# A fused attention and MLP kernel: weight splits tied to the MLP's steps, value halves at later steps

## The chip, the cores and the metric

One core of one Trainium2 chip runs the whole program. The metric is the device time of one launch in microseconds (us), and lower is better. The engines are named as in the profile: PE (TensorE matmuls), DVE (VectorE), ACT (ScalarE), POOL (GpSimd) and SP, which issues the transfers. Each engine works through its own instructions in the order in which they stand, so one that waits holds up all that stand behind it.

## What is computed

Attention within clusters: a query sees only those keys that the same centroid wins. Its result goes through a two-layer MLP with a squared ReLU.

```python
# q, k, v: (4, 8, 768, 64); centroids: (8, 16, 64); x: 3072 tokens of 512
q_n, k_n, c_n = (t / (norm(t) + 1e-6) for t in (q, k, centroids))
q_assign = argmax(einsum('bhsd,hcd->bhsc', q_n, c_n), -1)      # k_assign likewise
mask = q_assign[:, :, :, None] == k_assign[:, :, None, :]
attn = softmax(where(mask, q @ k.T / sqrt(64), -1e9))
x = (attn @ v) laid out as (3072, 512)
h = x @ w_in                                # w_in: 512 x 2048
out = (s * relu(h) ** 2 + b) @ w_out        # w_out: 2048 x 512
```

## The kernel before

To keep float32 accuracy on float16 matmuls, a tensor is split into a high half (the value rounded to float16) and a low half (what rounding left), and the products of the halves are added up in PSUM.

**The loop.** The main loop counts steps `i`. Attention has 192 units; a unit is one batch, one head and 128 queries against 768 keys. Step `i` makes the scores of unit `i` on PE (L516), their maximum on DVE (L526) and their exponentials on ACT (L536). Units 0 to 15 (`RAW`) are multiplied with unsplit values: PE transposes their exponentials (L560), and ACT and DVE copy the result out of PSUM (L140, L142). From unit 16 on `high` and `low` split the exponentials, the low half on POOL (L568), a transposing DMA turns them (L570), and `value` multiplies them with the value halves four steps later (L617 to L619). After 16 units a chunk of 256 tokens is complete (`finish_x`), and the MLP works on it 21 steps (`LAG`) behind: step `i` runs MLP step m = i - 21, that is pair `ft` = m mod 16 of chunk m div 16. `mlp_in` (L676) multiplies with the first layer's weights of that pair, `mlp_relu` takes the sum out of PSUM with ACT (L683, L685, L686), `mlp_gl` makes a low half on POOL (L691), and three steps on `mlp_out` (L703) multiplies with the second layer's weights.

**The weights.** 32 pieces of 512 KB (16 of each layer) are loaded in the first steps by `weights`: the load (SP, into three buffers called `stage` and a fourth place called `gs`), `rebase` (ACT, L244), `narrow` (DVE, L248 and L249), and `bound` (ACT, L256 and L258, and PE, L261), which gathers norms. When all 32 are through, `finish_w_in` and `finish_w_out` make the scales in `glob`, and only then `wsplit(ft)` can split pair `ft`: for each of its two tiles (`wis`, `wos`) ACT writes the high half (L307) and DVE the low half (L310). A split writes into one of 33 buffers, of which five are free at first, so the later splits wait for the low half of an earlier one, with which a raw weight's buffer comes free. `wsplit(ft)` is started in step 17 + ft.

**The value halves.** `prep_v(0)` splits the first batch's values, a pair of heads at a time (`halves`): ACT the high half (L223), DVE the low half (L225). The pair `hp` is let in from step 14 + 2 hp (`RAW - 2 + 2 * hp`), and first read at step 20 + 4 hp. The unsplit values stay in their buffers (`kv`, five in all) until then.

**What sets the order.** The functions only record instructions. A list scheduler with a timeline of its own puts them in order, engine by engine: what was recorded earlier goes first unless it isn't ready in that timeline, then something later fills in. `behind(x)` puts what is recorded under it behind `x` on the engine of `x`; it sets order and adds no wait for the end of `x`. `first_of_all` lifts the units 0 to 19 above the rest. In `wsplit` the pairs from `ft` = 4 on stand behind `first_x`, the last instructions of `finish_x` for the fourth group of units; the first four stand behind nothing.

## Time and profile before

| | us |
|---|---|
| median of 3 runs | 911.07 (909.8 to 915.86) |
| the profiled execution, its own time | 912.4 |
| its span, first to last instruction | 910.7 |
| PE busy | 830.3 (91%) |
| ACT busy | 712.7 (78%) |
| DVE busy | 631.2 (69%) |
| POOL busy | 544.0 (60%) |

The shares are averages over a start (some 220 us, in which the weights come in and the engines other than PE are full) and a long rest in which PE is nearly always busy. The page also shows that TensorE's clock was granted in full from 157.8 us on and was at times at half before. A time is read as microseconds from the span's start. "Busy" is the union of an engine's instruction times in a stretch; the idle time in brackets behind a row is that of its engine just before it, with what ended it.

### The profile page before, as it was taken

What the parts mean: (1) busy time and instruction counts of PE and PEld (TensorE: products, weight loads), DVE (VectorE), ACT (ScalarE), POOL (GpSimd) and SP (SyncE); (2) the same over time, 40 slices, a digit from 0 to 9 for tenths busy, and PEclk for the clock granted to TensorE, in tenths of its full rate; (3) what the DMA queues carried; (4) which work ended last, traced back from release to release, by engine and by line L of the source; (5) the groups of instructions that cost most, each with busy time, mean ns of one, the idle gap of its engine ahead of it and who ended that gap; (6) DMA issues with size and microseconds to landing.
All of it is one profiled execution on the core that took longest, in us unless ns stands there. A gap on an engine that the chain in (4) does not pass through costs nothing.

```text
span 910.7 us, 22840 instructions
## 1 busy us (share of the span) xinstructions
PE 830.3 (91%) x8625; PEld 591.9 (65%) x8625; DVE 631.2 (69%) x1673; ACT 712.7 (78%) x1406; POOL 544.0 (60%) x580
## 2 busy tenths in 40 slices
PE   1675786899999899999999999999999999999997
PEld 0564664566677667777667767677677777777764
DVE  8789789979778758766877667669777557564200
ACT  4579786867798779889888788988988788788553
POOL 3111024587687668768778667777876667676422
PEclk9977576999999999999999999999999999999999
DMA  5997624697998897989899989689988767676200
GB/s 151 245 287 239 205 49 91 163 178 163 182 181 140 182 209 139 175 158 180 175 180 190 181 152 185 154 150 207 177 156 171 140 124 173 117 149 132 59 24 23
DMA packets 437758, 144.23 MB, mean 158 GB/s; under 512 B 405392, under 2 KB 434064, under 8 KB 437648
## 3 DMA queue, kind: packets, MB, share of 16 engines
q1 hardware_dynamic: 437648, 142.78, 76.1%
q8 instruction: 67, 1.10, 0.5%
q14 instruction: 43, 0.35, 0.1%
HBM read 35.69 MB, written 6.29 MB: 46 GB/s over the span
## 4 chain that ended last, share of the span: by engine, by line
PE 44%; DVE 21%; DMA 14%; ACT 9%; issue 6%; POOL 3%; SPq 2%; DVEq 0%; ACTq 0%; POOLq 0%
PE h L676 15%; PE acc L703 14%; PE sc L516 7%; DMA kn<-in_k_dram 4%; DVE ssm L526 4%; DMA qn<-in_q_dram 4%; ACT p L536 2%; PE sc L617 2%; PE sc L619 2%; ACT ssm L533 2%; PE sc L618 2%; DMA vn<-in_v_dram 2%; DVE ka L225 2%; SPq L570 1%; POOL ph L568 1%
## 5 line engine op out<-in xcount | busy, mean ns | idle before, releaser
L568 POOL TENSOR_TENSOR ph<-p,ph 128x768 f16<-128x768 f32 x176 | 296.3, 1683 | 154.0 <-ACT ph L140 63.9
L676 PE MATMUL h<-xk,wis 128*128 128x256 f16 x2304 | 288.3, 274 | 5.1 <-DMA xk<-xn 2.3
L703 PE MATMUL acc<-wos,gs 128*128 128x512 f16 x1152 | 280.6, 379 | 2.0 <-DVE o L711 0.8
L676 PEld LDWEIGHTS <-wis 128*128 128x128 f16 x2304 | 222.9, 98 | 63.6 <-issue 6.3
L536 ACT ACTIVATE p<-sc,ssm,qsm 128x768 f32<-128x768 f32 x192 | 189.3, 986 | 4.3
L526 DVE TENSOR_REDUCE ssm<-sc 128x1 f32<-128x768 f32 x192 | 181.9, 947 | 6.3 <-PE sc L516 6.2
L691 POOL TENSOR_TENSOR gs<-r,gs 128x256 f16<-128x256 f32 x192 | 136.1, 710 | 64.3 <-ACT r L686 55.3
L703 PEld LDWEIGHTS <-gs 128*128 128x128 f16 x1152 | 104.4, 98 | 94.8 <-issue 1.1
L533 ACT ACTIVATE ssm<-ssm,lift,qsm 128x1 f32<-128x1 f32 x192 | 73.0, 381 | 83.2 <-DVE ssm L526 82.5
L140 ACT ACTIVATE ph<-p 128x768 f16<-128x768 f32 x164 | 137.2, 836 | 0.6
L683 ACT ACTIVATE r<-h,cf 128x256 f32<-128x256 f32 x192 | 89.1, 465 | 39.8 <-PE h L676 34.0
L617 PE MATMUL sc<-halves,PT 128*128 128x65 f16 x1032 | 113.0, 195 | 0.1
L618 PE MATMUL sc<-halves,PT 128*128 128x64 f16 x1032 | 112.9, 192 | 0.0
L619 PE MATMUL sc<-halves,PT 128*128 128x65 f16 x1032 | 112.6, 193 | 0.0
L516 PE MATMUL sc<-keys,QA 128*128 128x384 f16 x384 | 99.8, 341 | 12.8 <-ACT p L536 10.9
L516 PE MATMUL sc<-keys,QB 128*128 128x384 f16 x384 | 99.7, 341 | 8.3 <-DMA QB<-qb 8.3
L617 PEld LDWEIGHTS <-PT 128*128 128x128 f16 x1056 | 99.0, 97 | 11.9 <-DMA PT<-ph 0.8
L618 PEld LDWEIGHTS <-PT 128*128 128x128 f16 x1056 | 98.1, 99 | 11.6 <-issue 0.7
L619 PEld LDWEIGHTS <-PT 128*128 128x128 f16 x1056 | 98.3, 97 | 0.0
L686 ACT ACTIVATE r<-r 128x256 f32<-128x256 f32 x192 | 79.2, 413 | 4.0
L623 DVE TENSOR_SCALAR ssm<-sc 128x1 f32<-128x1 f32 x172 | 26.3, 153 | 80.5 <-PE sc L619 79.0
L685 ACT ACTIVATE gs<-r 128x256 f16<-128x256 f32 x192 | 78.6, 411 | 1.6
(191 smaller groups left out, 1104.7 us busy)
## 6 DMA issues: line engine op xcount, KB each, us to landing
wst<-in_moe_w_in_dram SPq DMA_DIRECT2D x16, 512.0 KB, 4.7
kn<-in_k_dram SPq DMA_DIRECT2D x16, 384.0 KB, 4.2
qn<-in_q_dram SPq DMA_DIRECT2D x24, 256.0 KB, 3.6
vn<-in_v_dram SPq DMA_DIRECT2D x16, 384.0 KB, 3.9
out_dram<-o SPq DMA_DIRECT2D x12, 512.0 KB, 3.3
wst<-in_moe_w_out_dram SPq DMA_DIRECT2D x8, 512.0 KB, 5.0
gs<-in_moe_w_out_dram SPq DMA_DIRECT2D x8, 512.0 KB, 5.8
PT<-ph SPq DMA_TRANSPOSE x176, 3.5
```

Source lines behind the costliest of these rows:

```text
L140: A.activation(dst, src, AF.Copy)
L516: last_score[0] = nc.tensor.matmul(sc[:, e, :HALF], X[:, col, :], y[:, h * S + e * HALF : h * S + (e + 1) * HALF], start=st, stop=not st)
L526: last_max[0] = V.tensor_reduce(SM[i // 4][:, 0, j : j + 1], U[i]["sc"], axis=AX.XY, op=ALU.max, negate=True)
L533: A.activation(bi, sm[:, 0, j : j + 1], AF.Identity, scale=u["scale"], bias=lift)
L536: last_exp[0] = A.activation(p.rearrange("p (a b) -> p a b", a=2), u["sc"], AF.Exp, bias=bi, scale=u["scale"], **total)
L568: G.tensor_tensor(u["ph"][:, 1, :], u["p"], u["ph"][:, 0, :], op=ALU.subtract)
L617: nc.tensor.matmul(o1, PT[:, kt, :], vh[:, h, kt, : D + 1], start=(kt == 0), stop=False)
L618: nc.tensor.matmul(o, PT[:, kt, :], vl[:, h, kt, :], start=False, stop=False)
L619: nc.tensor.matmul(o1, PT[:, T + kt, :], vh[:, h, kt, : D + 1], start=False, stop=(kt == T - 1))
L676: nc.tensor.matmul(ph[:, :CW], WSP[ft][0][:, wl, kt, :], XS[(b, c, kt)][:, :, xl, :], start=(i == 0), stop=(i == len(terms) - 1))
L691: G.tensor_tensor(g[:, 1, :], r, g[:, 0, :], op=ALU.subtract)
L703: nc.tensor.matmul(acc[:, t, :], g[:, gl, rows], WSP[ft][1][:, wl, :], start=(ft == 0 and gl + wl == 0), stop=(ft == NF - 1 and gl == 1))
```

## The change

Four things change.

1. The pairs from `ft` = 4 on: the high halves (ACT) stand behind the latest `mlp_relu` recorded (`last_relu`), the low halves (DVE) behind the latest maximum (`last_max`). Since `wsplit(ft)` starts in step 17 + ft and goes on in the next two, `wis` stands behind the relu of pair ft - 4 of the first chunk (ACT) and the maximum of unit 18 + ft (DVE), and `wos` one step behind it.
2. The pairs 1 to 3 stand behind the two copies that take the last unsplit unit's transposes out of PSUM (`last_copy`).
3. The value halves of the first batch are let in at the steps 16, 19, 22 and 25, behind the latest exponentials and the latest maximum.
4. The queries of the second half of the heads of chunk 1 are loaded into a `stage` buffer, no longer into one of the eleven `big` ones.

```diff
--- before.py
+++ after.py
@@ -73,7 +73,8 @@
 
 
     last_transpose = [None]
-    first_x = [None, None]
+    last_relu = [None]
+    last_copy = [None, None]
     last_turn = [None]
     last_qa = [None]
     last_qb = [None]
@@ -137,9 +138,8 @@
 
     def copy(eng, dst, src):
         if eng is A:
-            A.activation(dst, src, AF.Copy)
-        else:
-            eng.tensor_copy(dst, src)
+            return A.activation(dst, src, AF.Copy)
+        return eng.tensor_copy(dst, src)
 
     def scalar_in(src, name):
         every = const([P, 1], F32, name)
@@ -303,10 +303,10 @@
         made = []
         for w, f in ((wi[ft], glob[:, 2:3]), (wo[ft], glob[:, 5:6])):
             e = parts(weight_tile(f"w{'io'[len(made)]}s{ft}"))
-            with behind(*first_x[: 2 * (ft >= 4)]):
+            with behind(*([last_relu[0]] if ft >= 4 else last_copy if ft else ())):
                 A.activation(e[:, 0], w, AF.Copy, scale=f)
             yield
-            with behind(*first_x[: 2 * (ft >= 4)]):
+            with behind(*([last_max[0]] if ft >= 4 else last_copy if ft else ())):
                 V.scalar_tensor_tensor(e[:, 1], w, f, e[:, 0], op0=ALU.mult, op1=ALU.subtract)
             made.append(e)
         WSP[ft] = (made[0], made[1].rearrange("p e a f -> p e (a f)"))
@@ -392,7 +392,7 @@
     def prep_q(b, c, hq):
         n = f"{b}_{c}_{hq}"
         nh = 4
-        if b or c > 1:
+        if b or c > 1 or c + hq > 1:
             qn = sb.tile([P, CT * DM], F32, tag="stage", name=f"qn_{n}", bufs=3)
         else:
             qn = sb.tile([P, T * P], F32, tag="big", name=f"qn_{n}", bufs=BIGN)
@@ -479,7 +479,7 @@
         V.tensor_scalar(vm[:, 6:7], vm[:, 6:7], 2.0 ** -19, None, op0=ALU.mult)
         for hp in range(NP):
             if b == 0:
-                yield from until(RAW - 2 + 2 * hp)
+                yield from until(RAW + 3 * hp)
             if b == 1 and hp == 0:
                 yield from until(LAG + NF - 1)
             both = halves[:, (b * NP + hp) % 5]
@@ -487,7 +487,12 @@
             vl = both[:, VHW:].rearrange("p (h t d) -> p h t d", h=2, t=T)
             VS[(b, hp)] = (vh, vl)
             G.memset(vh[:, :, :, D:], 1.0)
-            yield from split(vh[:, :, :, :D], vl, vns[hp], vm[:, 7:8], False)
+            parted = split(vh[:, :, :, :D], vl, vns[hp], vm[:, 7:8], False)
+            with behind(*((last_exp[0], last_max[0]) if b == 0 else ())):
+                next(parted)
+            yield
+            with behind(*((last_exp[0], last_max[0]) if b == 0 else ())):
+                next(parted, None)
             if hp < NP - 1:
                 yield
                 if b > 0:
@@ -560,7 +565,9 @@
                     nc.tensor.transpose(turned[:, e, kt * P : (kt + 1) * P], u["p"][:, (e * n + kt) * P : (e * n + kt + 1) * P], ident)
                 cols = slice(e * n * P, (e + 1) * n * P)
                 if i < RAW:
-                    copy((V, A)[e], flat[:, cols], turned[:, e, : n * P])
+                    done = copy((V, A)[e], flat[:, cols], turned[:, e, : n * P])
+                    if i == RAW - 1:
+                        last_copy[e] = done
                 else:
                     A.activation(two[:, 0, cols], turned[:, e, : n * P], AF.Copy)
                     V.tensor_tensor(two[:, 1, cols], turned[:, e, : n * P], two[:, 0, cols], op=ALU.subtract)
@@ -636,9 +643,8 @@
         if hp == 0:
             XM[(b, c)] = sb.tile([P, 8], F32, tag="xm", name=f"xm_{g}", bufs=4)
         xn = sb.tile([P, CT, 2, 2, D], F16, tag="xn", name=f"xn_{g}", bufs=1)
-        made = [A.activation(xn[:, :, 0], xs, AF.Copy), absmax(XM[(b, c)][:, hp : hp + 1], xs.rearrange("p t h d -> p (t h d)"))]
-        if g == NP - 1:
-            first_x[:] = made
+        A.activation(xn[:, :, 0], xs, AF.Copy)
+        absmax(XM[(b, c)][:, hp : hp + 1], xs.rearrange("p t h d -> p (t h d)"))
         yield
         G.tensor_tensor(xn[:, :, 1], xs, xn[:, :, 0], op=ALU.subtract)
         x = xs_kept[:, g % 9]
@@ -680,7 +686,7 @@
         n = f"{b}_{c}_{ft}"
         ph = GS[(b, c, ft)]
         r = sb.tile([P, CW], F32, tag="r", name=f"r_{n}", bufs=2)
-        A.activation(r, ph[:, :CW], AF.Relu, scale=MS[(b, c)][0])
+        last_relu[0] = A.activation(r, ph[:, :CW], AF.Relu, scale=MS[(b, c)][0])
         g = gs[:, ft % 4]
         A.activation(g[:, 0, :], r, AF.Square)
         A.activation(r, r, AF.Square)
```

Nothing is computed otherwise than before. Where the instructions stand now, at three places:

ACT in the middle of the weights' preparation, before. `xs_0` and `xs_1` are results of the first units, `wo9`, `wi8` and so on are weight pieces, `wab` the work of `bound`, `PT_8` a copy of transposed exponentials:

```order
L635 ACTIVATE xs_0_663<-xs_0_663,vm_0_318 128x256
L223 ACTIVATE halves_131<-vn_0_0_319,vm_0_318 128x12x64
L223 ACTIVATE halves_131<-vn_0_1_443,vm_0_318 128x12x64
L223 ACTIVATE halves_131<-vn_0_2_511,vm_0_318 128x12x64
L223 ACTIVATE halves_131<-vn_0_3_588,vm_0_318 128x12x64
L244 ACTIVATE wo9_843<-gs_128 128x512
L140 ACTIVATE PT_8_916<-turned_138 128x384
```

and with the change:

```order
L642 ACTIVATE xs_0_663<-xs_0_663,vm_0_318 128x256
L244 ACTIVATE wo9_843<-gs_128 128x512
L141 ACTIVATE PT_8_916<-turned_138 128x384
L258 ACTIVATE wab_16_885<-wi8_790 128x512
L642 ACTIVATE xs_1_879<-xs_1_879,vm_0_318 128x256
L646 ACTIVATE xn_0_776<-xs_0_663 128x2x128
L256 ACTIVATE wab_17_899,l1_133<-wo8_798 128x512
```

The four high halves of the values are gone from here, and `wo9` with all behind it moves up by four instructions; on DVE the four low halves leave the same place.

ACT behind the exponentials of unit 18, before (`p_18`: exponentials, `wis4`, `wos4`: high halves of weights, `qb_0_1_1`: queries, `ssm`: bias of a maximum):

```order
L536 ACTIVATE p_18_1376<-sc_18_1367,ssm_16_1303,qsm_0_1_0_819 128x768
L533 ACTIVATE ssm_16_1303<-ssm_16_1303,lift_136,qsm_0_1_0_819 128x1
L223 ACTIVATE qb_0_1_1_1362<-qn_0_1_1_1222,qsm_0_1_1_1262 128x4x64
L639 ACTIVATE xn_3_1397<-xs_3_1332 128x2x128
L307 ACTIVATE wis4_1577<-wi4_542,glob_134 128x512
L307 ACTIVATE wos4_1634<-wo4_550,glob_134 128x512
L307 ACTIVATE wis5_1640<-keys_130,glob_134 128x512
L307 ACTIVATE wos5_1700<-keys_130,glob_134 128x512
L307 ACTIVATE wis6_1705<-keys_130,glob_134 128x512
L307 ACTIVATE wos6_1781<-wo6_684,glob_134 128x512
L307 ACTIVATE wis7_1785<-wi7_722,glob_134 128x512
L536 ACTIVATE p_19_1428<-sc_19_1419,ssm_16_1303,qsm_0_1_0_819 128x768
```

and with the change:

```order
L541 ACTIVATE p_18_1373<-sc_18_1364,ssm_16_1300,qsm_0_1_0_819 128x768
L646 ACTIVATE xn_3_1394<-xs_3_1329 128x2x128
L223 ACTIVATE qb_0_1_1_1359<-qn_0_1_1_1220,qsm_0_1_1_1259 128x4x64
L541 ACTIVATE p_19_1423<-sc_19_1414,ssm_16_1300,qsm_0_1_0_819 128x768
L223 ACTIVATE halves_131<-vn_0_1_443,vm_0_318 128x12x64
L538 ACTIVATE ssm_20_1465<-ssm_20_1465,lift_136,qsm_0_1_0_819 128x1 x2
L541 ACTIVATE p_20_1468<-sc_20_1436,ssm_20_1465,qsm_0_1_0_819 128x768
L689 ACTIVATE r_0_0_0_1555<-h_0_0_0_1542,cf_0_0_1538 128x256
L141 ACTIVATE ph_20_1528<-p_20_1468 128x768
L541 ACTIVATE p_21_1532<-sc_21_1502,ssm_20_1465,qsm_0_1_0_819 128x768
L307 ACTIVATE wis4_1571<-wi4_542,glob_134 128x512
L689 ACTIVATE r_0_0_1_1618<-h_0_0_1_1605,cf_0_0_1538 128x256
```

Seven weight splits stood between `p_18` and `p_19`. Now `p_19`, `p_20`, the first relu (`r_0_0_0`) and `p_21` come ahead of the first of them, and one pair stands there in each step.

DVE from the maximum of unit 27 to that of unit 28, before (all weights are split by then; `xs_6` is a unit's result, `vm_1` and `ka_1_0` are work on the next batch's values and keys):

```order
L526 TENSOR_REDUCE ssm_24_1747<-sc_27_1943 128x1
L119 TENSOR_REDUCE vm_1_1702<-vn_1_2_1859 128x1
L119 TENSOR_REDUCE xm_4_1707<-xs_5_1736 128x1
L225 SCALAR_TENSOR_TENSOR qa_0_2_0_1852<-qn_0_2_0_1636,qsm_0_2_0_1696,qb_0_2_0_1853 128x4x64 x2
L623 TENSOR_SCALAR ssm_24_1747<-sc_28_2017 128x1
L624 RECIPROCAL ssm_24_1747<-ssm_24_1747 128x1
L627 TENSOR_SCALAR xs_6_2042<-sc_28_2017,ssm_24_1747 128x64
L526 TENSOR_REDUCE ssm_28_2052<-sc_28_2017 128x1
```

and with the change:

```order
L531 TENSOR_REDUCE ssm_24_1744<-sc_27_1943 128x1
L310 SCALAR_TENSOR_TENSOR wos8_1939<-wo8_798,glob_134,wos8_1939 128x512
L310 SCALAR_TENSOR_TENSOR wis9_1941<-wi9_835,glob_134,wis9_1941 128x512
L120 TENSOR_REDUCE xm_4_1704<-xs_5_1733 128x1
L630 TENSOR_SCALAR ssm_24_1744<-sc_28_2017 128x1
L120 TENSOR_REDUCE vm_1_1699<-vn_1_3_1935 128x1
L142 CAST ph_27_2050<-p_27_1979 128x768
L631 RECIPROCAL ssm_24_1744<-ssm_24_1744 128x1
L329 TENSOR_REDUCE om_q0_2_0_2095<-pq_0_2_0_2078 128x8
L225 SCALAR_TENSOR_TENSOR ka_1_0_2006<-kn_1_0_1634,ksm_1_0_1855,ka_1_0_2006 128x12x64
L469 TENSOR_REDUCE amb_v1_2348<-vm_1_1699 128x1
L634 TENSOR_SCALAR xs_6_2042<-sc_28_2017,ssm_24_1744 128x64
```

Two weight splits (`wos8`, `wis9`) now stand behind this maximum, and two behind each of the next ones, up to `wos15` behind that of unit 34. Between the maxima of the units 20 and 24 three splits are left on DVE where fifteen stood before.

## Rows read from the trace of the kernel before

**Rows 1.** Windows: busy us (instructions) of PE, PEld, DVE, ACT, POOL; granted clock, DMA.
```profile
72.20:118.40 46.20, 32.23 (x189) 24.66 (x190) 38.74 (x97) 38.83 (x85) 5.43 (x6) 0.63 0.67 205
118.40:142.60 24.20, 16.84 (x111) 13.42 (x111) 21.09 (x60) 16.94 (x31) 9.10 (x8) 0.75 0.20 44
142.60:166.30 23.70, 18.89 (x164) 12.64 (x163) 23.57 (x42) 17.69 (x32) 11.06 (x9) 0.68 0.63 124
166.30:181.90 15.60, 12.55 (x125) 8.42 (x126) 15.60 (x38) 12.63 (x28) 7.71 (x8) 1.00 0.62 151
181.90:199.00 17.10, 15.65 (x190) 10.31 (x189) 14.27 (x32) 11.24 (x23) 13.50 (x14) 1.00 0.89 169
199.00:220.50 21.50, 19.96 (x207) 13.60 (x204) 16.59 (x53) 16.55 (x35) 14.98 (x15) 1.00 0.82 166
220.50:279.00 58.50, 57.85 (x633) 40.13 (x634) 42.39 (x113) 45.38 (x86) 43.69 (x45) 1.00 0.91 174
```

**Rows 2.** Windows of line L310 alone: DVE busy us (instructions), clock, DMA.
```profile
118.40:142.60 24.20, 8.75 (x12) 0.75 0.20 44
142.60:166.30 23.70, 15.14 (x15) 0.68 0.63 124
166.30:181.90 15.60, 5.64 (x6) 1.00 0.62 151
```

**Rows 3.** Timeline, ACT and PE, behind unit 18: start us, us, engine, line, names.
```profile
130.66 0.98 ACT L536 ACTIVATE p<-sc,ssm,qsm 128x768 f32<-128x768 f32 x1
134.32 0.71 ACT L307 ACTIVATE wis<-wi,glob 128x512 f16<-128x512 f32 x1
140.90 0.72 ACT L307 ACTIVATE wis<-wi,glob 128x512 f16<-128x512 f32 x1 [1.52 <-DVE wos L310]
141.53 0.97 ACT L536 ACTIVATE p<-sc,ssm,qsm 128x768 f32<-128x768 f32 x1
142.55 0.80 PE L516 MATMUL sc<-keys,QA 128*128 128x384 f16 x2 [4.28 <-ACT p L536]
```

**Rows 4.** Timeline, value halves on ACT and DVE, then SP's next load.
```profile
79.97 3.40 ACT L223 ACTIVATE halves<-vn,vm 128x768 f16<-128x768 f32 x4
81.97 1.95 DVE L225 SCALAR_TENSOR_TENSOR halves<-vn,vm,halves 128x768 f16<-128x768 f32 x2
88.17 0.52 SPq L91 DMA_DIRECT2D gs<-in_moe_w_out_dram  x1
```

**Rows 5.** Timeline, SP, DVE and ACT around the queries' transpose.
```profile
99.45 1.23 SPq L431 DMA_TRANSPOSE QA<-qa  x1
105.17 0.29 DVE L329 TENSOR_REDUCE om_q<-pq 128x8 f32<-128x128 f32 x1 [1.45 <-PE pq L441]
111.16 0.63 ACT L256 ACTIVATE wab<-wo 128x512 bf16<-128x512 f32 x1 [3.31 <-PE pw L261]
118.37 0.16 DVE L292 TENSOR_REDUCE amb_w<-l 128x1 bf16<-128x16 f32 x1
```

**Rows 6.** Timeline, two splits on DVE and a low half on POOL.
```profile
149.33 0.75 DVE L310 SCALAR_TENSOR_TENSOR wos<-wo,glob,wos 128x512 f16<-128x512 f32 x1
149.65 1.93 POOL L568 TENSOR_TENSOR ph<-p,ph 128x768 f16<-128x768 f32 x1 [9.53 <-ACT ssm L533]
150.19 1.93 DVE L310 SCALAR_TENSOR_TENSOR wis<-wi,glob,wis 128x512 f16<-128x512 f32 x1
```

**Rows 7.** Timeline, PE: one pair's mlp_in at half and at full clock.
```profile
150.88 2.75 PE L676 MATMUL h<-xk,wis 128*128 128x256 f16 x12
164.53 1.47 PE L676 MATMUL h<-xk,wis 128*128 128x256 f16 x12
```

**Rows 8.** Timeline, DVE: queries' low halves, a values' maximum, the maximum of unit 36.
```profile
143.22 0.87 DVE L225 SCALAR_TENSOR_TENSOR qa<-qn,qsm,qb 128x256 f16<-128x256 f32 x2
181.82 0.94 DVE L119 TENSOR_REDUCE vm<-vn 128x1 f32<-128x768 f32 x1
220.51 0.95 DVE L526 TENSOR_REDUCE ssm<-sc 128x1 f32<-128x768 f32 x1
```

## Prediction

> **What bounds the kernel now.** I read the windows first, with bounds at a few DVE instructions [rows 1]: the first is where the weights' scales begin (the maximum over their norms, at 118.37 [rows 5]), the others are the ends of the maxima of the units 20, 24, 27, 31 and 36. The reader should look for the engine that is full. Before 118.4 DVE and ACT are busy 38.7 and 38.8 of 46.2 us. From 118.4 to 181.9 DVE is busy 60.3 of 63.5 us, without a gap in its last 39 us, while PE is busy 48.3 and runs at half clock for much of it. From 181.9 on DVE has slack (30.9 of 38.6), PE is over 90% busy, and from 220.5 to 279.0 PE is busy 57.9 of 58.5. So there are three stages: the weights' preparation, which ACT, DVE and the loads share; a stage that DVE bounds, up to unit 27; and PE's stage, which is the rest of the program. From unit 27 to 36 a step takes (17.1 + 21.5) / 9 = 4.3 us.
>
> What fills DVE is the weight split: of its 60.3 us, 29.5 are L310 (33 entries, one counted twice at an edge, so 0.90 each) [rows 2]. ACT shows the other side of it: between the exponentials of the units 18 (130.66) and 19 (141.53) stand seven high halves, the last of which waits 1.52 us for DVE to free a buffer, and PE waits 4.28 us for unit 19's exponentials [rows 3].
>
> After the maximum of unit 36 both kernels have the same work left, and PE bounds it. I therefore work out when that maximum ends with the change, against 221.46 before (220.51 + 0.95 [rows 8]; the window ends at its start). Every difference there reaches the end in full.
>
> **The weights' preparation.** The change takes four high halves from ACT (3.40 us at 79.97) and four low halves from DVE (two of them 1.95 us at 81.97, so 3.9) [rows 4]. They stood ahead of `wo9`, whose end frees the buffer for the load at 88.17, so that load and the pieces behind it start earlier. Besides, SP issued the queries' transpose QA at 99.45 behind a weight load that waited for DVE; the scores' stage stands still on it, DVE waits 1.45 us for the product made from it at 105.17, and ACT 3.31 us at 111.16 for a norm queued behind it on PE [rows 5]. With the change SP has QA ahead of that load. Lower bound of the gain: 0, if the loads alone set the pace. Upper bound: the 3.9 us of DVE work plus the two waits' larger part, some 6 us. As DVE and ACT are at 84% there, I take nearly the ACT work itself: **3.5 us**, so the scales begin at 114.9. The `stage` buffer for the queries of chunk 1 costs nothing: the weights' last loads are through by then.
>
> **From there to unit 36**, window by window, DVE's work first. A split is 0.73 in the first window (8.75 / 12) and 0.90 later, a value half 0.95 [rows 4], two queries' low halves 0.8 (0.87 with what overlaps the next) and a maximum of the next batch's values 0.9 [rows 8].
> - 118.4 to 142.6, to unit 20: 21.1 busy before. Three splits leave (-2.2), one value half comes (+0.95), two queries' halves come (+0.8), a 0.7 us maximum has moved ahead: 19.9. The splits of pair 3 now stand in the wait for the first chunk's maximum, so 3.1 us of idle time shrink to 1.7: 21.6 us, before 24.2.
> - To unit 24: 23.6 busy before. Twelve of fifteen splits leave (-15.1 + 2.7), two value halves come (+1.9), the queries' go (-0.8): 12.2. DVE is no longer the bound. The four steps are bounded below by PE's pace, 4 x 4.3 = 17.2. From above they are bounded by PE at half clock, at which one `mlp_in` takes 2.75 us against 1.47 [rows 7]: four of them add 5.1, and scores and second layer not more than that again on the four steps that are mixed here: some 23.5. Clock is at half in much of this window before, and PE will be denser: I take 19.0, before 23.7.
> - To unit 27: 15.6 before; as many splits (6); a value half, a values' maximum and two queries' low halves come in (0.95 + 0.9 + 0.8): 18.2. DVE is full again: 18.6 us, before 15.6.
> - To unit 31: 14.3 before; eight splits come (+7.2); the maximum and the queries' halves go (-1.7), small work on keys and values comes from the next window (+1.2): 21.0 in all, with 1.1 idle 22.1 us, before 17.1.
> - To unit 36: 16.6 before; seven splits come (+6.3), that small work and a chunk's first numbers go (-1.6): 21.3, with 1.2 idle 22.5 us, before 21.5.
>
> The sum is 103.8 us against 102.1: 1.7 lost. The reason is plain: DVE's work up to unit 36 is 92.6 us against 91.1 (the splits only move, and the value halves are added), and now it has idle time early, in steps 20 to 24, which the pacing keeps it from filling, while the late steps, which DVE had slack in, become DVE's: 5.0 us a step against PE's 4.3. ACT's part of the splits (0.71 each [rows 3]) fits: 11.2 of 17.1 and 16.6 of 21.5 us were busy there. The splits' lateness costs PE nothing by itself: `wis10`, for one, stands behind the maximum of unit 28, and its first product stands behind the scores of unit 30.
>
> With the 3.5 us gained before, the end moves by **-1.8 us**. Against the profiled execution's own 912.4 us that is 910.6; that execution is 1.3 us above the median, and from the median it is 911.07 - 1.8 = **909.3 us**.
>
> **Price of a split beside POOL.** At 149.33 a low half takes 0.75 us; at 150.19, begun under a POOL low half of 1.93 us, the same takes 1.93 [rows 6]. POOL is busy 47% and 49% of the windows in which most splits stand now, and 79% and 70% of the two in which fifteen of them will stand [rows 1]. The 0.90 that I use holds some such meetings already; the bounds for the fifteen are 0.66 (start to start of splits that meet nothing: -3.6 us in all) and 1.93 (+15.5 us). I stay at 0.90, since a split behind an even unit's maximum comes before POOL's next low half is ready. The Trainium skill ("SBUF — State Buffer", section "Who interferes with whom") has a rule for it that speaks against the change: a DVE instruction with two inputs in SBUF and a GpSimd instruction that reads SBUF share a port, and whichever starts first holds it to its end. The pair of rows agrees with it, and by the rule alone the fifteen late splits would meet POOL more often than the others do, which is the third rival below.
>
> **The rivals.**
> 1. *The slack is used, faster.* Meetings stay rare (-0.24 x 15 = -3.6), steps 20 to 24 run at PE's pace (-1.8), the preparation gains 6 (-2.5), two thirds of the idle time in the last two windows go (-1.5): -9.4 from the forecast, **899.9**. For it: DVE idles 0.1 us in 39 when it is the bound. Against it: each piece must come out at its favourable end.
> 2. *PE's clock holds the early steps.* With the clock at half through steps 20 to 24 the 19.0 become 23.5: **913.8**. For it: clock 0.75 and 0.68 in these windows before. Against it: PE has more to do in a row than before.
> 3. *POOL meets the late splits, slower.* Half of the fifteen wait as at 150.19: 7.5 x 1.03 = +7.7, **917.0**; all of them, 924.8. It decides from about two in three on, where the time passes 1% above now. For it: POOL's 79% and 70%. Against it: at 47 to 49% the price was only some 0.2 per split above the clean one.
> 4. *The preparation isn't shorter*, since loads set it: +3.5, **912.8**, the change then doing in its first part nothing that counts.
>
> **How the numbers follow.** Forecast 0.45 (905 to 913), rival 1 0.23, rival 2 0.10, rival 3 0.12, rival 4 0.10. The range takes in the rivals up to the middle of 1 and of 3: 900 to 917.5. About 1%, 9.1 us, is what a measurement of this kernel can tell from no change: below 902.0 is most of rival 1 (0.18 with a little of the forecast), above 920.2 the far part of rival 3 and mixtures of 2 and 3 (0.08).
>
> **What would show it.** In the changed kernel's profile: the scales begin near 115 (118.4 now); the exponentials of unit 19 follow those of unit 18 within 4 us instead of 10.9; DVE has gaps between the maxima of the units 20 and 24 and almost none from 24 to 36, where a step takes some 5 us; the maximum of unit 36 begins near 219; L310's mean stays near 0.95 us. The forecast is wrong if DVE keeps gaps behind unit 27 (something else bounds, or the sum of its work is less than 92 us), if L310's mean passes 1.3, or if the start gains what I say and the steady steps behind unit 48 differ.

## The result, and the profile after

The changed kernel takes 925.64 us (median of 4 runs, 920.88 to 928.0) against 910.6 beside it: a ratio of 1.0143, interval 1.0114 to 1.0171. A second set of its runs gave 1.0122 (1.0082 to 1.0163). It is slower by 1.2 to 1.4%, where 909.3 us, no measurable change, was forecast. The profiled execution took 920.88 us.

The page after, TensorE's busy time and the clock granted to it in 40 slices:

```profile
PE 827.2 (90%) x8625; PEld 589.4 (64%) x8625; DVE 642.9 (70%) x1673; ACT 712.4 (78%) x1406; POOL 548.7 (60%) x580
PEclk9967689998999999999999999999999999999999
```

PE's busy time is 827.2 us, 3.1 less than before, in a span that is 8.5 longer: PE waits.

The windows of the start, with bounds as in [rows 1] (the scales, then the ends of the maxima of the units 20, 24, 27, 31 and 36):

```profile
72.20:112.40 40.20, 29.79 (x189) 22.67 (x188) 35.41 (x92) 35.76 (x83) 5.01 (x6) 0.69 0.81 236
112.40:132.10 19.70, 15.39 (x131) 12.21 (x130) 18.58 (x58) 13.46 (x23) 8.92 (x8) 0.86 0.24 55
132.10:148.50 16.40, 12.63 (x136) 8.65 (x133) 13.94 (x29) 12.03 (x24) 11.05 (x10) 0.90 0.74 138
148.50:169.90 21.40, 17.70 (x176) 11.86 (x175) 21.26 (x41) 17.12 (x36) 12.32 (x11) 1.00 0.71 166
169.90:190.40 20.50, 17.12 (x206) 11.99 (x205) 20.43 (x42) 16.61 (x32) 14.14 (x14) 1.00 0.59 131
190.40:216.10 25.70, 15.61 (x170) 10.12 (x167) 24.80 (x56) 18.79 (x37) 17.32 (x16) 0.95 0.58 136
```

DVE (the third pair) idles 2.5 us between the maxima of the units 20 and 24 and 1.1 us in all from there to unit 36: the picture that was forecast. Four lines of the timeline answer [rows 5], [rows 3] and [rows 8]: the scales, the exponentials of the units 18 and 19, the maximum of unit 36:

```profile
112.40 0.17 DVE L292 TENSOR_REDUCE amb_w<-l 128x1 bf16<-128x16 f32 x1 [0.68 <-ACT wab L256]
127.01 0.98 ACT L541 ACTIVATE p<-sc,ssm,qsm 128x768 f32<-128x768 f32 x1
128.59 0.99 ACT L541 ACTIVATE p<-sc,ssm,qsm 128x768 f32<-128x768 f32 x1
215.14 0.94 DVE L531 TENSOR_REDUCE ssm<-sc 128x1 f32<-128x768 f32 x1
```

So the start is better than forecast: that maximum begins 5.4 us before the one at 220.51 of [rows 8], where 1.8 were said (3.4 in the mean of the eight profiles below that have this start, against the five with the old one). And yet the end is 8.5 us later. To see where they go I compare, unit by unit, the start of PE's first score matmul (L516, with the change L521; four to a unit) in the profiled executions. Us against before, minus is ahead:

| profile | unit 36 | 42 | 48 | 54 | 84 | 121 | 191 |
|---|---|---|---|---|---|---|---|
| changed kernel | -10.0 | -2.9 | -3.1 | -4.2 | +2.8 | +8.3 | +8.5 |

Before, they start at 217.68, 246.11, 269.10, 293.87, 415.33, 565.72 and 840.98. Two things happen: a lead of ten becomes one of three at once, and between the units 54 and 121 some 12.5 us are lost, steadily and for good. From unit 121 on it hardly changes.

Windows of the first loss, from the scores of unit 36 to those of unit 42, before and then with the change; PE is the first pair after the length, the granted clock the third number from the end:

```profile
217.68:246.11 28.43, 27.23 (x286) 17.49 (x284) 20.85 (x58) 20.68 (x39) 20.45 (x21) 1.00 0.93 192
207.71:243.21 35.50, 29.56 (x294) 19.42 (x292) 27.98 (x66) 23.49 (x44) 22.90 (x23) 0.90 0.80 157
```

Of the 7.1 us between them 4.7 are waits of PE, and 2.3 are PE's busy time: its clock, in full there before, was granted at half (1.2 GHz) from 213.6 to 220.4. It fell within two waits of PE, of 1.56 and 2.82 us, with 0.6 us of products between them (their rows stand with the last experiment).

Windows of the second loss, with bounds at the first scores of the units 54, 66, 75, 87, 105 and 121; PE is the first pair after the length. Before:

```profile
293.87:343.85 49.98, 47.02 (x504) 33.00 (x502) 33.17 (x84) 39.60 (x78) 32.27 (x33) 1.00 0.95 188
343.85:380.57 36.72, 36.72 (x416) 26.66 (x416) 29.93 (x89) 32.64 (x65) 27.34 (x26) 1.00 0.93 170
380.57:426.48 45.91, 45.91 (x530) 32.81 (x528) 28.55 (x87) 40.08 (x79) 35.41 (x35) 1.00 0.82 156
426.48:501.10 74.62, 72.44 (x826) 52.06 (x822) 58.45 (x150) 63.93 (x126) 56.77 (x61) 1.00 0.94 184
501.10:565.72 64.62, 63.21 (x705) 44.79 (x702) 43.27 (x121) 52.59 (x104) 45.63 (x46) 1.00 0.89 166
```

With the change:

```profile
289.68:342.92 53.24, 50.88 (x527) 35.54 (x526) 36.94 (x95) 41.10 (x80) 32.80 (x33) 1.00 0.90 182
342.92:380.49 37.57, 33.51 (x393) 24.22 (x392) 27.61 (x79) 30.93 (x63) 26.98 (x27) 1.00 0.82 159
380.49:428.65 48.16, 45.48 (x506) 32.21 (x504) 29.38 (x83) 38.35 (x75) 33.72 (x34) 1.00 0.74 143
428.65:503.17 74.52, 71.90 (x840) 52.13 (x837) 56.13 (x152) 63.37 (x125) 56.01 (x60) 1.00 0.89 177
503.17:573.99 70.82, 65.20 (x711) 45.46 (x709) 49.69 (x125) 54.53 (x108) 47.42 (x47) 1.00 0.80 166
```

The five add up to 271.9 us with PE idle 6.6, and to 284.3 with PE idle 17.3. Of the 12.5 us that are lost 10.8 are waits of PE; its work is the same within 1.7. Up to unit 66 PE idles no more than before; it only does more of its products early, which are missing in the next windows. The added waits lie behind. Of what PE waits for, the view of waits names, before (294 to 564 us; us in total, times, longest):

```profile
PE sc L516 <- DMA QB<-qb: 2.8, 2, 1.8
PE h L676 <- DMA xk<-xn: 2.3, 1, 2.3
```

and after (290 to 571 us):

```profile
PE h L682 <- ACT r L689: 3.3, 2, 2.7
PE sc L521 <- ACT p L541: 2.4, 4, 1.4
PE pk L386 <- DMA keys<-ka: 2.1, 1, 2.1
PE am_q L116 <- DVE ssm L630: 1.6, 2, 1.0
PE h L682 <- DVE oe_k L330: 1.4, 1, 1.4
```

A few waits for transposes have become many for ACT, DVE and the keys. No line of code of that stretch was changed. But the order of its instructions was: of PE's 3613 matmuls from the scores of unit 40 up to those of unit 121, 581 stand behind another unit's scores than before; from there on the order is the same but for one. For example, what stands on PE behind the scores of a unit, in counts of matmuls (`h`: first layer, `acc`: second, `pq`: queries, `am`: small maxima; the 18 value products left out):

```
unit   before                              changed
61     6 acc, 12 h                         16 pq, 12 h
62     6 acc, 12 h                         10 acc, 21 h
63     6 acc, 12 h                         3 h
64     6 acc, 12 h, 2 am                   2 am, with 14 acc and 12 h between its two halves of scores
71     12 h, 6 acc, 12 h                   1 h, with 11 h ahead of the value products
82     12 h, 8 acc, 2 h, 4 acc             5 acc
```

In the units 61 to 64 an even 18 MLP products each have become bunches and short units. In a short unit PE comes sooner to the next scores or the next `h`, for which ACT must have made room; in these four units that cost a wait of 0.5 us, the longer ones come from unit 69 on.

### The profile page after: what moved, and what is told of

Its sections match the earlier page's. It is cut to its first block, busy times and chain, and to the rows that moved or that the text cites. A ratio compares the mean times of both kernels' runs of the same rounds, so it can differ in the third digit from the quotient of the medians.

```text
span 919.2 us, 22818 instructions
## 1 busy us (share of the span) xinstructions
PE 827.2 (90%) x8625; PEld 589.4 (64%) x8625; DVE 642.9 (70%) x1673; ACT 712.4 (78%) x1406; POOL 548.7 (60%) x580
## 5 line engine op out<-in xcount | busy, mean ns | idle before, releaser
L709 PE MATMUL acc<-wos,gs 128*128 128x512 f16 x1152 | 283.5, 379 | 5.7 <-DVE o L717 2.4
L521 PE MATMUL sc<-keys,QA 128*128 128x384 f16 x384 | 99.3, 339 | 12.3 <-ACT p L541 9.1
L521 PE MATMUL sc<-keys,QB 128*128 128x384 f16 x384 | 99.5, 341 | 7.9 <-DMA QB<-qb 7.9
L625 PEld LDWEIGHTS <-PT 128*128 128x128 f16 x1056 | 97.9, 99 | 11.4 <-issue 0.5
L626 PEld LDWEIGHTS <-PT 128*128 128x128 f16 x1056 | 98.1, 97 | 0.0
L630 DVE TENSOR_SCALAR ssm<-sc 128x1 f32<-128x1 f32 x172 | 26.3, 153 | 91.7 <-PE sc L626 90.6
```

Source lines behind the costliest of these rows:

```text
L521: last_score[0] = nc.tensor.matmul(sc[:, e, :HALF], X[:, col, :], y[:, h * S + e * HALF : h * S + (e + 1) * HALF], start=st, stop=not st)
L625: nc.tensor.matmul(o, PT[:, kt, :], vl[:, h, kt, :], start=False, stop=False)
L626: nc.tensor.matmul(o1, PT[:, T + kt, :], vh[:, h, kt, : D + 1], start=False, stop=(kt == T - 1))
L709: nc.tensor.matmul(acc[:, t, :], g[:, gl, rows], WSP[ft][1][:, wl, :], start=(ft == 0 and gl + wl == 0), stop=(ft == NF - 1 and gl == 1))
```

## The experiments

Two theories to begin with. The first: the redrawn order of the rest is what costs, whatever the start. The second, a rival: the start hands over something worse (late data, full buffers), whatever the order. To tell them apart an order is pinned, engine by engine, with a loop at the end of the program; it adds no wait for an end, just as `behind` doesn't:

```diff
+    for engine, packed in PINNED.items():
+        mine = [x for x in recorded if str(x.engine) == "EngineType." + engine]
+        steps_on = array.array("h", zlib.decompress(base64.b85decode(packed)))
...
+            if last_ is not None:
+                tc.add_manual_dep(mine[at_], last_.name, mybir.DependencyInfo(mybir.DependencyClass.NoSync, mybir.DependencyReason.DATA), reason="issue_after")
+            last_ = mine[at_]
```

`PINNED` holds a list of instructions for each engine; the runs below say what list. The pins by themselves cost nothing that shows: where a pinned kernel keeps the old order behind the old start, it stays within 0.7 us of before (up to unit 54, and with the new order from 87 on up to unit 87). The positions of the profiles, as in the table above, in us against the first profile of before. Each is one execution, and the one that they are compared with (912.4 us) is shorter than the medians of before beside these runs (913.74 to 915.31), so that the last column overstates a price; the ratios give it.

| profile | unit 36 | 48 | 54 | 84 | 121 | 191 |
|---|---|---|---|---|---|---|
| new start, old rest | -7.2 | -0.4 | -0.2 | +2.3 | +4.6 | +7.7 |
| old start, new rest | +1.1 | +1.5 | +0.5 | +12.1 | +16.2 | +18.2 |
| pace alone | -9.2 | -2.7 | -3.7 | +4.5 | +9.0 | +9.4 |
| halves alone | -3.0 | -2.4 | -2.6 | +9.2 | +14.2 | +14.4 |
| queries' buffer alone | 0.0 | +4.9 | +4.3 | +3.4 | +3.5 | +3.5 |
| old start, new order 54 to 86 | -0.3 | -0.3 | -0.3 | +7.7 | +10.7 | +12.4 |
| old start, new order 87 to 120 | -0.5 | -0.3 | -0.3 | -0.7 | +4.4 | +5.2 |
| old start, new order on PE alone | -0.2 | +0.1 | -0.1 | +22.6 | +25.1 | +25.3 |
| changed, old order 53 to 87 | -4.8 | +2.1 | +1.0 | +0.3 | +7.1 | +7.2 |
| new start, old order from 54 | -7.6 | -0.3 | -1.4 | -2.3 | -1.6 | +0.4 |
| the same, start pinned | -8.7 | -2.5 | -3.6 | -2.4 | -1.1 | +1.4 |
| changed kernel again | -5.9 | +0.5 | -0.5 | +6.0 | +11.3 | +11.4 |
| changed, one key step later | -9.5 | -2.4 | -3.5 | +4.3 | +10.3 | +10.5 |
| start pinned, two DVE steps later | -6.7 | +0.1 | -1.0 | -1.3 | +0.5 | +0.6 |

**Start and rest crossed.** The changed kernel, and the kernel before, each with the other's order from step 40 on:

```diff
 # in the changed kernel
+PINNED = the order of before, from the scores of unit 40 on
 # in the kernel before
+PINNED = the order of the changed kernel, from the scores of unit 40 on
```

> The changed kernel, but from step 40 on every engine's instructions are put in the order in which they stand in the kernel before (an order only, no waits are added). Theory 1, the order of the rest costs: the start keeps its gain (maximum of unit 36 near 215, 220.5 before) and the rest its old pace, so the time is 910.6 - 5.4 = about 905. Theory 2, the state in which the new start hands over costs, whatever the order: the loss between the steps 60 and 120 stays, and the time is 918 to 926.

> The kernel before, but from step 40 on every engine's instructions are put in the order in which they stand in the changed kernel. Theory 1, the order of the rest costs: the maximum of unit 36 at 220.5 as before, then some 14 us lost up to step 120: about 924 to 930. Theory 2, the handover costs: no loss, about 911.

New start with the old order: 913.49 us, ratio 0.9999 (0.9974 to 1.0025). Old start with the new order: 929.36, ratio 1.0153 (1.0100 to 1.0207). So the order costs 1.2 to 1.5% behind either start, and the first theory holds in what it says of the order. In what it says of the start it fails: the 5.4 us were not kept, 905 us did not come, and the start by itself is worth nothing that can be measured. The second loses its time between the units 54 and 121, the stretch in which the changed kernel does. (The profile of the first is a long execution, 920.1 us.)

**Parts of the change alone.** The first and second part; the third; the fourth:

```diff
-            with behind(*first_x[: 2 * (ft >= 4)]):
+            with behind(*([last_relu[0]] if ft >= 4 else last_copy if ft else ())):
```
```diff
-                yield from until(RAW - 2 + 2 * hp)
+                yield from until(RAW + 3 * hp)
```
```diff
-        if b or c > 1:
+        if b or c > 1 or c + hq > 1:
```

> The change with the value halves back at the steps 14, 16, 18, 20 and the queries back in a big buffer: the pacing of the weight splits alone. Its order from step 40 on is that of the changed kernel, instruction for instruction. Theory 1: its own gain up to unit 36 (I expect the weights' scales at 118 as before, and 0 to 3 us of gain from there), then the same 14 us of loss: 921 to 927. Theory 2: the loss differs from that of the changed kernel, since the handover does.

> The kernel before with the value halves alone moved to the steps 16, 19, 22 and 25. Its order from step 40 on is that of the changed kernel too, though no weight split is paced. Theory 1: the scales begin some 4 to 6 us earlier (112 to 114), the splits run as before, the maximum of unit 36 comes 3 to 6 us earlier, and then 14 us are lost: 919 to 924. Theory 2: the handover is near the old one, so there is no such loss: about 906.

> Of the change only the fourth part, the queries of chunk 1 in a stage buffer; the order from unit 58 on is that of before. Theory 1: the order of the rest is what costs, so without it no change, 909 to 913. Rival, the buffer itself costs something (a later load of these queries, a buffer that is missing for the weights): 914 or more.

922.85 us (1.0089, 1.0053 to 1.0126), 924.22 (1.0111, 1.0074 to 1.0147) and 915.73 (1.0011, 0.9988 to 1.0034). With the pace alone or the halves alone the order from step 40 on is, instruction for instruction, that of the whole change; with the buffer alone it is that of before from unit 58 on. The price comes with the order, not with a part: two edits that share nothing cost alike, and together hardly more. The gain in the preparation goes with the halves: in the three profiles, one each, the scales begin at 117.78 (pace), 115.39 (halves) and 118.61 (buffer), 118.37 before.

**Where in the rest.** The kernel before with the new order in one stretch only, and the changed kernel with the old order in one:

```diff
+PINNED = before's order from unit 40 on, but the changed kernel's from 54 to 86
+PINNED = before's order from unit 40 on, but the changed kernel's from 87 to 120
 # in the changed kernel:
+PINNED = its own order from unit 40 on, but before's from 53 to 87
```

> The kernel before, its whole order from step 40 on pinned to its own, but for the stretch from the scores of unit 54 to those of unit 87, where the instructions stand as in the changed kernel (the second batch's preparation of its later chunks and the third batch's keys lie in it). Theory 1, the order in this stretch carries most of the loss: with the old start and the new rest the maxima ran +11 us from unit 54 to 84 and kept it, so 910.6 + 9 to 12 = 920 to 923, the maximum of unit 84 some 10 us late and the difference constant from there on. Rival, the loss is spread over the whole rest or hangs on what is carried into the stretch: under 914. Second rival, the loss is made up later because PE has slack behind it: unit 84 late, the end below 914.

> The kernel before, pinned as in the last one, but with the changed kernel's order from the scores of unit 87 to those of unit 121 instead. Theory 1, each batch's preparation loses by its own order: in the runs with the new rest the maxima lost 3 to 5 us between the units 102 and 120, so 913.5 to 916. Rival, the second loss is a consequence of the first (what was late from 54 to 86 arrives later): 910.6, no change.

> The changed kernel with its own order from step 40 on, but with that of before from the scores of unit 53 to those of unit 88. The mirror of the run with only this stretch new (1.0068). Theory 1: PE idles no more from unit 66 to 87, 8 us come back, and what stays is the loss from unit 105 to 121 less the start's lead: ratio 1.001 to 1.006. Rival, the loss hangs on the way into the stretch or comes back behind it: 1.010 or more.

923.19 us (1.0068, 1.0043 to 1.0093), 918.33 (1.0022, 1.0004 to 1.0039) and, for the mirror, 918.35 (1.0036, 1.0015 to 1.0056). The loss lies in two stretches. Put in alone, the one in which the third batch's keys and the second's last queries are prepared costs 0.7%, and the next 0.2%; both are less than expected (1.010 to 1.014 and 1.003 to 1.006 of the time before), and together less than the 1.2 to 1.5% of the whole order. With the first one taken out of the changed kernel 0.4% are left. So most of the loss is in the first; whether the two add up to the whole the intervals don't tell. Windows of the mirror, from the scores of unit 66 to 75, 75 to 87 and 105 to 121:

```profile
344.14:380.87 36.73, 36.73 (x417) 26.68 (x417) 29.99 (x89) 32.70 (x65) 27.37 (x26) 1.00 0.91 167
380.87:426.77 45.90, 45.90 (x530) 32.79 (x528) 28.73 (x87) 40.10 (x79) 35.17 (x35) 1.00 0.83 158
502.86:572.78 69.92, 65.20 (x711) 45.45 (x709) 49.63 (x127) 54.55 (x108) 47.27 (x47) 1.00 0.79 169
```

With the old order PE doesn't idle at all in the first two, though it comes from the new start; in the last, which keeps the new order, it still idles 4.7 us.

**PE's order alone.**

```diff
+PINNED = before's order from unit 40 on, but on PE the changed kernel's from 54 to 120
```

> The kernel before with its own order pinned from step 40 on, and from the scores of unit 54 to those of unit 121 the changed kernel's order on PE alone; the other engines keep theirs. Theory 3, PE's own order makes the loss (MLP products bunched in some units and missing in others, so that PE waits for exponentials and relus): ratio 1.009 or more, PE idle some 15 us from unit 54 to 121. Theory 4, what costs is the order on DVE and SP (steps of the next batch's preparation that stand in front of a maximum and wait for a load): under 1.005. A price above the changed kernel's 1.014 would say that the two orders don't fit each other, which tells the theories apart no further.

938.97 us, 1.0273 (1.0239 to 1.0307): far more than the change. PE waits above all for relus (293 to 600 us):

```profile
PE h L676 <- ACT r L683: 6.2, 6, 2.3
```

From unit 90 on it loses nothing more. From unit 54 to 90 PE's clock, too, was at half four times. As the expectation says, a price above the change's tells that the orders don't fit each other; it doesn't settle whether PE's own bunches or the other engines' places are to blame. The opposite mix was not run.

**One instruction moved.** PE's longest wait with the change is 2.68 us in front of an `h` at 409.14. The timeline, backward from it (PE, ACT, DVE, DVE, SP):

```profile
409.14 1.03 PE L682 MATMUL h<-xk,wis 128*128 128x256 f16 x8 [2.68 <-ACT r L689]
408.34 0.39 ACT L538 ACTIVATE ssm<-ssm,lift,qsm 128x1 f32<-128x1 f32 x1 [5.58 <-DVE ssm L531]
407.36 0.95 DVE L531 TENSOR_REDUCE ssm<-sc 128x1 f32<-128x768 f32 x1
406.03 0.96 DVE L120 TENSOR_REDUCE amb_k<-kn 128x1 bf16<-128x768 f32 x1 [2.74 <-DMA kn<-in_k_dram]
399.60 0.57 SPq L92 DMA_DIRECT2D kn<-in_k_dram  x1
```

and before (DVE, SP):

```profile
402.02 0.95 DVE L119 TENSOR_REDUCE amb_k<-kn 128x1 bf16<-128x768 f32 x1 [0.32 <-DMA kn<-in_k_dram]
397.86 0.57 SPq L91 DMA_DIRECT2D kn<-in_k_dram  x1
```

The `h` needs the place of an older one, whose relu stands on ACT behind the bias of unit 80, that behind the maximum of unit 80 on DVE, and that behind a step for the third batch's keys, which waits for their load. In both kernels the step stands in front of that maximum; before, its load had all but landed. With the change SP sends it 1.74 us later, and the step begins 4.0 us later; the rest is the load, which took longer (6.4 us from issue to step, 4.2 before), and why is not shown. If that is the cause, the step behind the maximum should take the wait away:

```diff
 the changed kernel's order, DVE:
-amb_k2_1 <- kn_2_1
 ssm_76 (reciprocal)
 xs_19
 ssm_80 <- sc_80 (maximum)
+amb_k2_1 <- kn_2_1
```

> The changed kernel with one instruction moved on DVE: the maximum over the third batch's second keys (amb_k2_1) stands behind the maximum of unit 80 instead of in front of it. Theory 4 for the longest wait of PE (2.68 us at 406.46 for a relu): DVE waited 2.67 us for the keys' load there and the maximum of unit 80 behind it; with the move PE's wait shrinks to 0.7 or less, and the step from the maximum of unit 78 to that of 84 takes 24 to 24.5 us instead of 26.2. The end comes 2 us earlier, a ratio of 1.012. Rival, PE waits there for the unit's own order whoever comes first: the step stays at 26.

> The changed kernel unaltered, as the measure for the one-instruction move on the same chip: 1.014 of before, the step from unit 78 to 84 some 26 us, PE's wait of 2 to 3 us for a relu in it.

With the move 926.2 us, 1.0135 (1.0105 to 1.0166); the changed kernel beside it 923.77, 1.0122. The wait is gone. From the scores of unit 78 to those of 84 it takes 23.1 us (25.9 in the unmoved kernel's new profile, 23.0 before); by the maxima, which stand behind such steps themselves, 25.2 against 26.3. But from unit 84 to 90 it then takes 26.6 against 24.6 (25.4 in the first profile of the change), and PE shows a wait that the unmoved kernel doesn't have there:

```profile
432.64 0.20 PE L624 MATMUL sc<-halves,PT 128*128 128x65 f16 x1 [1.67 <-DMA PT<-ph]
```

So the cause of this one wait is shown. Of the 2.8 us that are won, 1.1 to 1.9 are given back six units later, but from the scores of unit 78 to those of unit 121 the moved kernel's profile still loses 6.2 us against before, where both profiles of the unmoved one lose 8.3: the 2 us that were expected. It is not ahead at the end, since it had lost 4.5 us from unit 66 to 78, ahead of the move (0.8 and 0.9 in the others), with the clock at half from 358.5 to 365.3. In the medians the gain does not show: 0.2% is less than their intervals can tell.

**Whether the start's lead can be kept.** The new start up to unit 54 with the old order behind it; the same with every instruction of the start pinned too; and that with two DVE steps of the next batch (low halves of its first values and of its second keys) moved behind the maximum of unit 36:

```diff
+PINNED = in the changed kernel, before's order from the scores of unit 54 on
+PINNED = the changed kernel's own order up to there, then before's
 # the same, on DVE:
-halves <- vn_1_0
-ka_1_1 <- kn_1_1
 ssm_32 <- sc_35 (maximum)
 ssm_36 <- sc_36 (maximum)
+halves <- vn_1_0
+ka_1_1 <- kn_1_1
```

> The changed kernel with its own order up to unit 54 and the order of before from the scores of unit 54 on. At unit 54 the changed kernel was 5.3 us ahead, against 0.2 ahead where the old order began at step 40. Theory 1, the start's gain reaches the end once the order behind it is the old one: 910.6 - 5 = 905 to 907. Rival, what is gained ahead of a stage that PE bounds is given back in that stage whatever its order: 910 to 914, the lead gone by unit 84.

> As the kernel with the new start and the old order from unit 54, but with every instruction ahead of unit 54 pinned to the changed kernel's own order (there the start had shifted a little). Theory 1, the start's lead (5.3 us at unit 54 in the changed kernel's profile) reaches the end behind the old order: ratio 0.993 to 0.996. Rival, a lead is given back in the stage that PE bounds, whatever its order: 0.998 to 1.002, the lead at unit 132 under 2 us.

> The kernel with the new start and, from unit 54 on, the old order, with two instructions moved on DVE: the low halves of the next batch's first values and of its second keys (halves from vn_1_0, ka_1_1) stand behind the maximum of unit 36, no longer in front of that of unit 35. In the new start PE leads by 8.7 us at the scores of unit 36 and by 2.3 at those of unit 42; it waits 2.8 us for the queries' transpose and 3 us for the MLP's own numbers between them, all behind this DVE work, and its clock is granted at half for some us after. Theory 5, this work in front of the two maxima loses the lead: PE's waits there shrink by 3 us or more, the lead at unit 42 is 5 us or more, ratio 0.994 to 0.997 (the kernel without the move was 0.999). Rival, DVE is simply full there, and what is moved holds up the next maxima or the keys of unit 37 instead: lead at 42 under 3.5 us, ratio 0.998 to 1.001.

913.12 us (0.998, 0.9957 to 1.0002), 913.0 (0.999, 0.9967 to 1.0012) and 913.89 (0.9982, 0.9961 to 1.0004): all three the same as before within their intervals, and none a version that beats it; the theory that expects a gain falls each time. In each profile the lead of 6.7 to 8.7 us at the scores of unit 36 shrinks by 6.4 to 7.5 up to those of unit 42. With the change PE waits there for these:

```profile
210.62 0.61 PE L709 MATMUL acc<-wos,gs 128*128 128x512 f16 x2 [1.56 <-ACT gs L691]
214.04 0.19 PE L440 MATMUL pq<-cT,QA 128*128 128x16 f16 x1 [2.82 <-DMA QA<-qa]
```

and with the two steps moved:

```profile
216.36 0.18 PE L440 MATMUL pq<-cT,QA 128*128 128x16 f16 x1 [1.91 <-DMA QA<-qa]
224.87 0.20 PE L624 MATMUL sc<-halves,PT 128*128 128x65 f16 x1 [1.71 <-DMA PT<-ph]
```

The wait for `gs` stays at 1.55, one shrinks by 0.9, another of 1.7 comes. The theory that those two steps lose the lead falls; the rival, a DVE that is full there, fits (24.80 of 25.70 us busy in the window up to unit 36). The clock takes its part: between the units 36 and 42 it was at half for 3.4 to 10.2 us in each of the eight profiles with the new start, and never in the five with the old one. It goes with the paced splits: the profile of the pace alone shows it too (6.8 us), those of the halves and of the buffer alone don't.

## Why the prediction was wrong

**The step that failed** is the sentence "After the maximum of unit 36 both kernels have the same work left, and PE bounds it", with what it concludes: "Every difference there reaches the end in full." The work is the same, but not its order, and in a stage in which PE is busy over 97% of the time an order is worth more than the whole start. The crossed runs show it: 1.2 to 1.5% for the order, 0.0% for the start. The order was there to be read before the run, and I read it at three places only, all ahead of unit 36. The forecast did name, as a sign that it was wrong, a start that gains as said with other steady steps behind unit 48. That is what came, but it stood in no rival and in no term of the range.

**A second part of that sentence failed too**: the maximum of unit 36 is not the point from which PE alone decides. PE led by 10.0 us at its scores and by 2.9 six units on: behind a DVE that was still full it waited 4.7 us more than before, and 2.3 more went with its clock at half. What a start is worth should be read where the engine that bounds the rest runs without waits, here from unit 48.

**The terms of the start were near, in part by luck.** By one profile the scales begin at 112.40, a gain of 6.0 where 3.5 was taken; over the eight profiles with this start they begin at 114.3 in the mean (112.40 to 117.39), over five with the old one at 118.1 (117.74 to 118.42): 3.8 us. From the scales to the maximum of unit 36 it took 102.7 us, where the sum said 103.8. Window by window it was 19.7, 16.4, 21.4, 20.5 and 24.7 up to the start of that maximum, against 21.6, 19.0, 18.6, 22.1 and 22.5: the errors cancel, and DVE had more to do, 98.1 us (99.0 less that maximum) against 92.6, most of it in the windows to the units 27 and 36 (3.1 and 2.6 us). In the preparation what was said came: the queries' transpose goes out at 91.95, not 99.45, and neither of the two waits of [rows 5] is left. At the scores of unit 48 the eight profiles are 0.75 us ahead in the mean and the five of the old start 0.2 behind: a lead of 0.9, where 1.8 was forecast. Between single profiles of one start it varies by over 5 us, so that the first one's 3.1 says little.

**The signs.** Exponentials of unit 19: 1.6 us after those of unit 18, within the 4 that were named. DVE's gaps: where they were said. A step from unit 24 to 36: 5.6 us, about 5 was said. L310's mean over all splits: 1.01 us, near 0.95 was said.

**The rivals.** The clock at half in the early steps: 0.90 granted up to unit 24, and that window took 16.4 us, not 23.5; for those steps it fell, but the clock cost its 2.3 us later, behind unit 36. Late splits that meet POOL: windows of L310 alone with the change (busy us of DVE and instructions; one stands in both)

```profile
169.90:190.40 20.50, 9.04 (x9) 1.00 0.59 131
190.40:216.10 25.70, 8.75 (x7) 0.95 0.58 136
```

make 17.8 us for the fifteen late splits, 1.19 each. The sum had 0.90, so this term was too small by 4.3 us, over half of what the rival took; it is most of DVE's added work, and other terms that came out smaller hid it. Seven of the fifteen took 0.74, and single meetings are as dear as in [rows 6]; one of the last splits, with POOL's row first:

```profile
201.38 2.12 POOL L575 TENSOR_TENSOR ph<-p,ph 128x768 f16<-128x768 f32 x1
201.92 2.12 DVE L310 SCALAR_TENSOR_TENSOR wis<-wi,glob,wis 128x512 f16<-128x512 f32 x1
```

The Trainium skill ("SBUF — State Buffer", section "Who interferes with whom") says that such a pair shares a port which the first to start holds; this pair agrees with it, the split taking 2.12 us where its neighbour, begun at 201.26 ahead of POOL's, took 0.74. The price of such meetings didn't decide the time.

**What stays open**: which engine's new places make the waits from unit 54 on. PE's bunches stand beside them, and one wait was traced through ACT and DVE to a load, but PE's order alone cost more than the change, so the orders can't be priced engine by engine.

## What to carry to other kernels

Where a scheduler draws the order, an edit at one place is two changes: the one in the diff, and a new order for everything behind it that nobody asked for; here the second cost 1.2 to 1.5% and the first was worth 0.0 to 0.2%. So list the order of the whole program before and after, and where it differs behind the edit, pin the old one before judging the edit, or give the redrawn order a term in the range. And read the worth of a start not at its last instruction but some units later, where the engine that bounds the rest no longer waits for the others, and over several profiles.

## What the hardware showed that was not expected

A wait of PE can cost twice, and its length alone doesn't tell which one will. From unit 121 on the old order runs nearly alike in every profile but for one place, at unit 144, where PE waits for a transpose of queries. A window of 5 us there (PE's busy time is the first pair, its granted clock the third number from the end), and the next first-layer products in the timeline, before:

```profile
655.00:660.00 5.00, 3.38 (x39) 2.38 (x38) 2.83 (x4) 4.97 (x10) 3.70 (x5) 1.00 0.96 214
```

```profile
658.62 1.47 PE L676 MATMUL h<-xk,wis 128*128 128x256 f16 x12
```

and, window and timeline, with the new start pinned and the old order from unit 54 on:

```profile
655.00:660.00 5.00, 2.88 (x27) 2.28 (x28) 2.05 (x3) 4.31 (x8) 4.83 (x5) 0.73 1.16 247
```

```profile
658.61 2.49 PE L682 MATMUL h<-xk,wis 128*128 128x256 f16 x12
```

PE waited 1.62 us before and 2.40 here; the clock stayed in full (2.4 GHz) in the one and fell to its lower level (1.2 GHz) for a part of the other, where the next twelve products took 2.49 us, not 1.47. The loss from unit 144 to 150 was 2.4 us for 0.8 us of longer waiting. But with the new order from 54 to 86 alone PE waited the same 2.40 us there, was busy the same 2.88 us in the window that begins as far (0.76 us) behind the start of unit 144's scores, and the clock stayed in full:

```profile
667.79:672.79 5.00, 2.88 (x36) 2.26 (x37) 1.72 (x3) 4.58 (x8) 4.82 (x5) 1.00 1.18 232
```

```profile
670.80 1.47 PE L676 MATMUL h<-xk,wis 128*128 128x256 f16 x12
```

That kernel lost 0.8 us from unit 144 to 150, the longer wait and nothing more; the other 1.6 are the clock's. The same shows at the keys' transpose: PE waited 2.07 us with the change, and the clock stayed at 1.00; with the one step moved it waited 2.88, and the next window ran at half; with the pace alone it waited 2.07 too, and the clock fell (0.72 in the window). PE's longest wait with the change, the 2.68 us in front of the `h` at 409.14, left it in full. What decides is not shown. The window at the keys' transpose with the change, then with the step moved:

```profile
360.00:365.00 5.00, 5.00 (x50) 3.47 (x48) 2.81 (x9) 2.50 (x6) 3.86 (x5) 1.00 0.64 147
```

```profile
360.00:365.00 5.00, 5.00 (x31) 2.66 (x30) 1.73 (x6) 1.71 (x3) 1.92 (x3) 0.50 0.51 114
```

PE is "busy" 5.00 us in both, with 50 products begun in the one and 31 in the other. So a busy share alone hides this cost; the clock beside it doesn't.
